# A mixer kernel's first loads: the 128 columns of x move from ACT's DMA queue to SP's

## The chip, the cores and the metric

The kernel runs on one core of a Trainium2 chip. The metric is the device time of one execution in microseconds (us); several executions are given by their median. The profile is that of one further execution.

The core has five engines that matter here: TensorE (PE), VectorE (DVE), ScalarE (ACT), GpSimd (POOL) and SyncE (SP). SP and ACT issue the loads and stores of this kernel, each on a queue of its own; in the profile SP's queue is q1 and ACT's is q10. The packets of both are moved by the same 16 DMA engines.

## The reference

The input x has 2048 rows of 512 bf16 values. Two branches read it, and a gate mixes them:

```python
# branch A: sliding, dilated local attention (32 heads of 16, 8 taps, 2 apart)
qkv = x @ wqkv                       # wqkv: 512 x 1536
logits = einsum(q, k[pos - 2*w]) * 16 ** -0.5     # w = 0..7, masked before the start
a = (softmax(logits) . v[pos - 2*w]) @ wo
# branch B: token mixing
h = layernorm(x)
u = gelu(h^T @ w1 + b1)              # w1: 2048 x 1792
b = (u @ w2 + b2)^T
# gate
g = sigmoid((x * gate_w).sum(-1))
out = g * a + (1 - g) * b
```

## The kernel before, in words

All of x, its transpose XT, the projections and the weights in use lie in one arena in SBUF. The work is written down as a list of operations, each with an engine, a planned duration, what it reads and writes, and at places an order by hand. A planner (`_Sched`) then puts the operations of each engine in order, with planned times, and works out which semaphores each must wait for. Each engine runs its own list in that order. Only the order and the waits reach the chip; the planned times do not.

The stages on TensorE follow one another:

- L536: warm-up matmuls on a constant, which nobody reads.
- L544: four small matmuls against an identity matrix. They transpose the 128 columns of x for the first 512 rows. ACT (`ev_tra`, L553) copies two results into XT, VectorE (`ev_trb`, L555) the other two.
- L617: the projections Q, K and V, 512 rows of x at a time ("blocks" 0 to 3). A result of 128 x 512 is the sum of four matmuls, one for each quarter of the 512 columns of x, which are the rows of Wq, Wk or Wv. ACT copies the results out (L625, L628).
- L696: sums over heads for the attention logits, from products that VectorE makes (L688).
- L810 and L860: the two big products of branch B. L876: the product with wo, whose results VectorE mixes into the output (L897).

For block 0 the eight results of Q and K lie in eight PSUM banks at once, and the loop goes over the quarters first: four matmuls (one for each quarter of Q's output) with column quarter 0 of x and the first quarter of Wq, then four with quarter 1, and so on, then Wk in two halves. So the first four matmuls need only 128 columns of x and 128 rows of Wq.

These 128 columns of block 0 come another way than the rest. The rest of block 0, columns 128 to 511, comes by a DMA that transposes on the way (`d_xt0`, L473). The first 128 columns come as a plain load, `d_xp` (512 rows of 256 bytes), into the tile OUTS, and TensorE transposes them (L544).

The first loads are, in the order in which they are issued before the change:

- on ACT's queue: `d_xp`, then the first quarter of Wq (`d_wp0_0`);
- on SP's queue: `d_xt0`, the other quarters of Wq (`d_wp0_1`, `d_wp0_2`, `d_wp0_3`), two halves of Wk (`d_wp1_0`, `d_wp1_2`), rows of x for the layer norm (`d_x0`), the transposing DMA of block 1 (`d_xt1`, L460), and then more of x, XT, Wv and w1.

Plain loads are issued at L429, through `mk_dma`. The loads on SP are kept in their order by `prev_dma()`: each is ordered behind the one before it. From `d_x2` on, `throttle()` makes each wait for the landing of the load five places ahead in the list `init_dmas`. The first loads carry planned landing times, set by hand, which stand in for the planner's own model of a DMA:

```python
for op_, t_ in zip(first_loads, (3.4, 4.6, 5.0, 5.4, 5.8, 6.6, 7.4, 8.2, 10.6)):
    op_.lands = t_
    op_.deps.clear()
d_xp.lands = 3.1
first_loads[0].order.add(d_xp)
```

`first_loads[0]` is the first quarter of Wq and `first_loads[1]` is `d_xt0`. The last line orders the quarter of Wq behind the columns of x on ACT's queue.

VectorE's whole order and parts of ACT's are written out as chains further down; the large matmuls of PE are one chain through `last_main`.

Of the kernel before, what the change touches and what calls it, by code (L numbers as in the profile page):

```python
# [333 lines left out]
def bass_gated_mix__sliding_local_dilated__mixer_token_mlp__prompt_kernel(nc, A_x, A_wqkv, A_wo, B_x, B_w1, B_b1, B_w2, B_b2, gate_w, out, dbg=None):  # L334
    with contextlib.ExitStack() as es:
# [3 lines left out]
        sch = _Sched()  # L339

        x2d = A_x[0]
        xv = x2d.rearrange("(t p) d -> p t d", p=128)
# [85 lines left out]
        def mk_dma(dst, src):  # L428
            return lambda e: e.dma_start(dst, src)  # L429
# [3 lines left out]
        def throttle():  # L433
            return [init_dmas[-5]] if len(init_dmas) >= 5 else []

        def prev_dma():
            return [init_dmas[-1]] if init_dmas else []

        def ld_x(t0, n, q="sp"):
            ds = sch.dsem("x%d" % t0)  # L440
            op = sch.dma(q, mk_dma(X[:, t0:t0 + n, :], xv[:, t0:t0 + n, :]), n * 128 * D * 2, ds,
                         writes=["x%d" % t for t in range(t0, t0 + n)], deps=throttle() if q == "sp" else [], after=prev_dma() if q == "sp" else [], name="d_x%d" % t0)
            if q == "sp":
                init_dmas.append(op)
            return op

        def ld_w(tn, d0, n, q="sp"):
            ds = sch.dsem("wqkv%d_%d" % (tn, d0))
            op = sch.dma(q, mk_dma(WQKV[:, d0:d0 + n, tn * D:(tn + 1) * D], wqkv_v[:, d0:d0 + n, tn * D:(tn + 1) * D]),
                         n * 128 * D * 2, ds, writes=["wqkv%d_%d" % (tn, dt) for dt in range(d0, d0 + n)],  # L450
                         deps=throttle() if q == "sp" and n == 4 else [], after=prev_dma() if q == "sp" else [],
                         issue=0.65 if n == 4 else 0.45, name="d_wp%d_%d" % (tn, d0))
            if q == "sp":
                init_dmas.append(op)
            return op
# [14 lines left out]
        def ld_xt0():  # L470
            ds = sch.dsem("xt0")
            dst = XT[:, 1:4, 0:512]
            op = sch.dma("sp", lambda e: e.dma_start_transpose(dst, x2d[0:512, 128:512]), 512 * 384 * 2, ds, issue=1.25,  # L473
                         writes=XT0[1:4], after=prev_dma(), name="d_xt0")
            init_dmas.append(op)
            return op

        XP = view("OUTS", BF16, [(128, 4), (1, 128)])
        d_xp = sch.dma("act", mk_dma(XP, xv[:, 0:4, 0:128]), 512 * 128 * 2, sch.dsem("xp"), writes=["outs0"], issue=0.4, name="d_xp")

        first_loads = [ld_w(0, 0, 1, "act"), ld_xt0(), ld_w(0, 1, 1), ld_w(0, 2, 1), ld_w(0, 3, 1), ld_w(1, 0, 2), ld_w(1, 2, 2),
                       ld_x(0, 2)]
        ld_xt(1)
        first_loads.append(init_dmas[-1])
        for op_, t_ in zip(first_loads, (3.4, 4.6, 5.0, 5.4, 5.8, 6.6, 7.4, 8.2, 10.6)):
            op_.lands = t_
            op_.deps.clear()
        d_xp.lands = 3.1
        first_loads[0].order.add(d_xp)
        init_dmas[:] = [first_loads[1]] + first_loads[5:]  # L490
        ld_x(2, 2)
        ld_x(4, 4)
# [7 lines left out]
        def ld_w1(j):  # L500
# [4 lines left out]
            if j < 4:  # L505
# [8 lines left out]
                       writes=["wo"], deps=throttle(), after=prev_dma(), name="d_wo")  # L514
# [4 lines left out]
        for i_, (v_, n_) in enumerate(((B_b1, NFT), (B_b2, NST))):  # L519
            vr = v_.rearrange("(t q j) -> q t j", q=4, j=32)  # L520
            for q_ in range(4):
                sch.dma("sp", mk_dma(psub(BR, 32 * q_, n_, 32 * i_, [(1, 32)]), vr[q_]), n_ * 64, ds_b, reads=["br"],
                        writes=["br_%d_%d" % (i_, q_)], deps=throttle(), after=prev_dma(), name="d_b_%d_%d" % (i_, q_), issue=0.45)
        d_w1.append(ld_w1(3))
        A("dve", lambda e: e.transpose(out=BT, in_=BR), 0.2, reads=["br_%d_%d" % (i_, q_) for i_ in range(2) for q_ in range(4)],
          writes=["btc"], name="t_b")
# [13 lines left out]
        def f_tr(h):  # L540
# [13 lines left out]
          writes=["xt0_0"], name="ev_tra", prio=0)  # L554
        A("dve", lambda e: e.tensor_copy(out=XT[:, 0, 256:512], in_=ps[:, 6, 0:256]), 0.35, reads=["lg6_0", "lg6_1"],  # L555
          writes=["xt0_0b"], name="ev_trb", prio=0)
# [76 lines left out]
        for (b0, d0, d1, s0, s1) in ((0, 0, 1, 0, 512), (0, 1, 2, 0, 512), (0, 2, 3, 0, 512), (0, 3, 4, 0, 512), (4, 0, 2, 0, 512), (4, 2, 4, 0, 512)):  # L633
            for b in range(b0, b0 + 4):
# [3 lines left out]
                                 writes=fbn[b], after=[last_main[0]], name="pf_%s%d_%d_%d" % (tnames[tn], dl, d0, s0))  # L638
                last_main[0].order.add(w3_)
        for b, (tn, dl) in enumerate(first):  # L640
            A("act", f_evq(tn, dl, 0, b), 0.52, reads=fbn[b] + (["k5pad"] if tn == 1 else []),
              writes=["%s5_%d_0" % (tnames[tn], dl)], name="ev_%s%d_0" % (tnames[tn], dl), prio=0)
# [7 lines left out]
        for (tn, dl, sb) in seq_proj:  # L650
# [4 lines left out]
                             writes=["acc%d" % bank], after=[last_main[0]], name="pj_%s%d_%d" % (tnames[tn], dl, sb), prio=0)  # L655
            A("act", f_evq(tn, dl, sb, bank), 0.62, reads=["acc%d" % bank] + (["k5pad"] if tn == 1 else ["v5pad"] if tn == 2 else []),
              writes=["%s5_%d_%d" % (tnames[tn], dl, sb)], name="ev_%s%d_%d" % (tnames[tn], dl, sb), prio=0)
# [11 lines left out]
                writes=["xa"] + ["wqkv%d_%d" % (tn, dt) for tn in range(3) for dt in range(4)], name="d_xa")  # L669
        for t in range(NST):  # L670
# [5 lines left out]
          writes=["th"], name="g_tanh", prio=0)  # L676
# [31 lines left out]
        for wh in range(2):  # L708
# [6 lines left out]
            for (dl, c0, nc_) in pieces:  # L715
# [5 lines left out]
                  writes=wr, name="qkm_%d_%d_%d" % (wh, dl, c0), prio=0)  # L721
            rd = sum([pbn(b_) for b_ in bufs], []) + PBX[wh] + ["rp"]
            for wl in range(4):
                qop = A("pe", f_qkr(list(enumerate(bufs)), (wl,)), 0.92, reads=rd, writes=["lg%d_0" % (4 + wl), "lg%d_1" % (4 + wl)],
                        name="qkr_%d_%d" % (wh, wl), prio=-100 + wl, delay=BURST_DELAY)
                A("act", (lambda wh_, wl_: (lambda e: e.activation(out=ATT[:, :, 4 * wh_ + wl_, :], in_=ps[:, 4 + wl_, :].rearrange("p (h c) -> p h c", h=2), func=AF.Copy)))(wh, wl),  # L726
                  0.55, reads=["lg%d_0" % (4 + wl), "lg%d_1" % (4 + wl)], writes=["lw%d" % (4 * wh + wl)],
                  name="lev_%d_%d" % (wh, wl), prio=0)
# [60 lines left out]
        for k_, u in enumerate(USEQ):  # L789
# [7 lines left out]
            for (nm, n_, du) in (("ava", 4, 2.25), ("avb", 2, 1.2)):  # L797
                A("dve", (lambda pv_, n__: (lambda e: e.tensor_tensor(out=pv_[:, 0:n__], in0=pv_[:, 0:n__], in1=pv_[:, n__:2 * n__], op=ALU.add)))(pv, n_),  # L798
                  du, writes=[pn], name="%s_%d" % (nm, u))
# [27 lines left out]
        for ft in range(NFT):  # L827
# [6 lines left out]
              name="gel_%d" % ft, prio=0)  # L834
# [84 lines left out]
        for i in range(NST):  # L919
# [4 lines left out]
            elif i > 1:  # L924
# [6 lines left out]
              name="t1_%d" % i, prio=0)  # L931
# [119 lines left out]
```

## Time and profile before

| | before |
|---|---|
| times of three runs | 169.61, 170.71, 167.72 us (median 169.61) |
| the profiled execution: time | 168.55 us |
| the profiled execution: span | 167.3 us |
| TensorE busy | 162.1 us, 97% of the span |
| VectorE busy | 151.3 us, 90% |
| ACT busy | 75.1 us, 45% |
| DMA packets on q1 (SP) | 45120 |
| DMA packets on q10 (ACT) | 2496 |

The span runs from the first to the last instruction of the profiled execution; its time also holds what lies around them. Times in the profile count from the span's start. A line of the profile gives the engine, the source line (L429), the operation and what it writes and reads; SPq and ACTq are the instruction streams of SP and ACT, in which DMAs are issued. The time that a DMA's issue takes there is not the time until its data has landed, which is given apart.

### The profile page before, as it was taken

What the parts mean: (1) busy time and instruction counts of PE and PEld (TensorE: products, weight loads), DVE (VectorE), ACT (ScalarE), POOL (GpSimd) and SP (SyncE); (2) the same over time, 40 slices, a digit from 0 to 9 for tenths busy, and PEclk for the clock granted to TensorE, in tenths of its full rate; (3) what the DMA queues carried; (4) which work ended last, traced back from release to release, by engine and by line L of the source; (5) the groups of instructions that cost most, each with busy time, mean ns of one, the idle gap of its engine ahead of it and who ended that gap; (6) DMA issues with size and microseconds to landing.
All of it is one profiled execution on the core that took longest, in us unless ns stands there. A gap on an engine that the chain in (4) does not pass through costs nothing.

```text
span 167.3 us, 2136 instructions
## 1 busy us (share of the span) xinstructions
PE 162.1 (97%) x845; PEld 77.5 (46%) x859; DVE 151.3 (90%) x154; ACT 75.1 (45%) x116; POOL 0.7 (0%) x8
## 2 busy tenths in 40 slices
PE   7699999999999999999999999999999999999994
PEld 2355555554454444444444444444444444444463
DVE  1055999999999999999999999999999999999896
ACT  3077688889899818793131121131231321310100
POOL 1000000000000000000000000000000000000000
PEclk9999999999999999999999999999999999999999
DMA  5999999959003846996779926462672570000454
GB/s 135 327 268 216 314 316 290 303 165 308 2 0 97 311 116 179 307 290 155 181 189 340 339 76 142 113 187 71 181 218 83 138 223 0 0 0 0 157 190 159
DMA packets 47625, 29.64 MB, mean 177 GB/s; under 512 B 9856, under 2 KB 46464, under 8 KB 47616
## 3 DMA queue, kind: packets, MB, share of 16 engines
q1 hardware_dynamic: 45120, 24.85, 54.4%
q10 hardware_dynamic: 2496, 4.66, 10.2%
q8 instruction: 7, 0.11, 0.3%
q14 instruction: 2, 0.02, 0.0%
HBM read 21.24 MB, written 2.10 MB: 140 GB/s over the span
## 4 chain that ended last, share of the span: by engine, by line
PE 91%; DMA 3%; DVE 2%; ACT 2%; issue 1%; ACTq 0%
PE ps L860 29%; PE ps L810 29%; PE ps L617 23%; PE ps L876 6%; PE ps L696 4%; DMA arena<-in_A_wqkv_dram 3%; DVE arena L897 2%; ACT L585 1%; ACT arena L628 1%; ACTq L429 0%; ACT arena L585 0%
## 5 line engine op out<-in xcount | busy, mean ns | idle before, releaser
L860 PE MATMUL ps<-arena 128*128 128x512 bf16 x220 | 48.5, 379 | 0.2
L810 PE MATMUL ps<-arena 128*128 128x512 bf16 x219 | 48.2, 379 | 0.4 <-issue 0.2
L617 PE MATMUL ps<-arena 128*128 128x512 bf16 x188 | 41.4, 379 | 1.6 <-DMA arena<-in_A_wqkv_dram 1.3
L688 DVE TENSOR_TENSOR arena<-arena 128x4096 bf16<-128x4096 bf16 (+1 forms) x12 | 35.5, 2998 | 2.5 <-ACT arena L628 2.1
L795 DVE TENSOR_TENSOR arena<-arena 128x8192 bf16<-128x8192 bf16 x8 | 35.0, 4419 | 0.0
L860 PEld LDWEIGHTS ps<-arena 128*128 128x128 bf16 x224 | 21.9, 98 | 26.4
L810 PEld LDWEIGHTS ps<-arena 128*128 128x128 bf16 x224 | 21.8, 98 | 26.6 <-ACT arena L726 0.4
L617 PEld LDWEIGHTS ps<-arena 128*128 128x128 bf16 x192 | 21.6, 113 | 21.5 <-issue 1.8
L928 ACT ACTIVATE arena<-ps,arena 128x512 bf16<-128x512 f32 x16 | 12.5, 778 | 39.4 <-PE ps L860 39.4
L798 DVE TENSOR_TENSOR arena<-arena 128x4096 bf16<-128x4096 bf16 (+1 forms) x16 | 27.0, 1751 | 0.0
L628 ACT ACTIVATE arena<-ps 128x512 bf16<-128x512 f32 x32 | 18.6, 596 | 4.5 <-PE ps L617 4.5
L831 ACT ACTIVATE arena<-ps,arena 128x512 bf16<-128x512 f32 x14 | 9.6, 687 | 22.2 <-PE ps L810 16.6
L572 DVE BATCH_NORM_STATS2 arena<-arena 128x6 f32<-128x512 bf16 x16 | 10.0, 682 | 6.1 <-DMA arena<-in_A_x_dram 6.1
L876 PE MATMUL ps<-arena 128*128 128x512 bf16 (+1 forms) x79 | 14.1, 336 | 0.1
L897 DVE SCALAR_TENSOR_TENSOR arena<-ps,arena 128x512 bf16<-128x512 f32 (+1 forms) x20 | 11.5, 637 | 0.9 <-PE ps L876 0.7
L596 ACT ACTIVATE arena<-arena 128x512 bf16<-128x512 bf16 x16 | 12.2, 804 | 0.0
L625 ACT ACTIVATE arena<-ps 128x512 bf16<-128x512 f32 x16 | 9.0, 597 | 6.2 <-PE ps L617 6.1
L876 PEld LDWEIGHTS ps<-arena 128*128 128x128 bf16 x80 | 7.8, 98 | 6.2
L672 DVE SCALAR_TENSOR_TENSOR arena<-arena 128x512 bf16<-128x512 bf16 x16 | 10.1, 689 | 0.0
L742 DVE TENSOR_TENSOR arena<-arena 128x512 bf16<-128x512 bf16 (+4 forms) x11 | 7.3, 667 | 0.6 <-ACT arena L761 0.2
L696 PE MATMUL ps<-arena 128*32 128x512 bf16 x128 | 7.3, 380 | 0.0
L726 ACT ACTIVATE arena<-ps 128x512 bf16<-128x512 f32 x8 | 4.7, 592 | 4.6 <-PE ps L696 4.6
(42 smaller groups left out, 40.0 us busy)
## 6 DMA issues: line engine op xcount, KB each, us to landing
arena<-in_B_w_dram SPq DMA_DIRECT2D x7, 1024.0 KB, 8.5
arena<-in_B_w_dram SPq DMA_DIRECT2D x8, 896.0 KB, 5.2
arena<-arena ACTq DMA_DIRECT2D x32, 128.0 KB, 2.9
arena<-in_A_x_dram SPq DMA_DIRECT2D x4, 512.0 KB, 6.1
out_dram<-arena SPq DMA_DIRECT2D x14, 128.0 KB, 1.7
arena<-in_A_x_dram SPq DMA_DIRECT2D x1, 1536.0 KB, 7.9
arena<-in_A_wqkv_dram SPq DMA_DIRECT2D x2, 256.0 KB, 3.8
arena<-in_A_x_dram SPq DMA_DIRECT2D x2, 256.0 KB, 3.6
```

The source lines that it names most:

```text
L596: A("act", (lambda t_: (lambda e: e.activation(out=X[:, t_, :], in_=X[:, t_, :], func=AF.Identity, scale=col(RSTD, t_), bias=col(NMR, t_)) ...
L617: ins = e.matmul(ps[:, bank, s0:s1], lhsT=lhsT, rhs=XT[:, dt, sb * 512 + s0:sb * 512 + s1], start=(dt == 0 and s0 == 0), stop=(dt == 3))
L628: return lambda e: e.activation(out=dst, in_=ps[:, bank, :], func=AF.Copy)
L688: return lambda e: e.tensor_tensor(out=PBL[buf][:, :, 512 * c0:512 * (c0 + nc_)], in0=in0, in1=in1, op=ALU.mult)
L696: ins = e.matmul(ps[32 * c:32 * c + 32, 4 + wl, :], lhsT=RP, rhs=PBL[buf][:, wl, c * 512:(c + 1) * 512], start=(dl == 0), stop=(dl == 3), ...
L795: A("dve", (lambda o_, i0, i1: (lambda e: e.tensor_tensor(out=o_, in0=i0, in1=i1, op=ALU.mult)))(pv, in0, in1), 4.4, reads=v_res + ["atx_% ...
L798: A("dve", (lambda pv_, n__: (lambda e: e.tensor_tensor(out=pv_[:, 0:n__], in0=pv_[:, 0:n__], in1=pv_[:, n__:2 * n__], op=ALU.add)))(pv, n ...
L810: ins = e.matmul(ps[:, bank, :], lhsT=W1W[:, slot, st, 128 * e_:128 * e_ + 128], rhs=X[:, st, :], start=(st == 0), stop=(st == NST - 1))
L860: ins = e.matmul(ps[:, bank, :], lhsT=W2S[slot][:, ft, 128 * e_:128 * e_ + 128], rhs=UT[:, ft, :], start=(ft == 0), stop=(ft == NFT - 1))
L876: ins = e.matmul(ps[:, bank, 0:c1 - c0], lhsT=OT[:, t, 128 * i:128 * i + 128], rhs=WO[:, t, c0:c1], start=(t == 0), stop=(t == 3))
L897: A("dve", (lambda i_, b_, c0_, c1_: (lambda e: e.scalar_tensor_tensor(out=T1[:, i_, c0_:c1_], in0=ps[:, b_, 0:c1_ - c0_], scalar=col(G, i ...
L928: A("act", (lambda i_, bank_: (lambda e: e.activation(out=T1[:, i_, :], in_=ps[:, bank_, :], func=AF.Identity, scale=col(OMG, i_), bias=co ...
```

## The change

`d_xp` is issued by SP instead of ACT, and `d_xt0` (`first_loads[1]`) is ordered behind it. The first quarter of Wq is then the only one of these loads on ACT's queue and has no load ahead of it. The planned landing of the Wq quarter goes from 3.4 to 3.0; those of the eight loads behind `d_xp` on SP go up by 0.3 each. Nothing else is changed.

```diff
         XP = view("OUTS", BF16, [(128, 4), (1, 128)])
-        d_xp = sch.dma("act", mk_dma(XP, xv[:, 0:4, 0:128]), 512 * 128 * 2, sch.dsem("xp"), writes=["outs0"], issue=0.4, name="d_xp")
+        d_xp = sch.dma("sp", mk_dma(XP, xv[:, 0:4, 0:128]), 512 * 128 * 2, sch.dsem("xp"), writes=["outs0"], issue=0.4, name="d_xp")
...
-        for op_, t_ in zip(first_loads, (3.4, 4.6, 5.0, 5.4, 5.8, 6.6, 7.4, 8.2, 10.6)):
+        for op_, t_ in zip(first_loads, (3.0, 4.9, 5.3, 5.7, 6.1, 6.9, 7.7, 8.5, 10.9)):
             op_.lands = t_
             op_.deps.clear()
         d_xp.lands = 3.1
-        first_loads[0].order.add(d_xp)
+        first_loads[1].order.add(d_xp)
         init_dmas[:] = [first_loads[1]] + first_loads[5:]
```

## The prediction

> **What bounds the kernel now.** I read the chain of work that ended last first, in order of time, then the waits of PE, then the table of stages, the timeline of the first six microseconds and the DMA landings of single issues.
>
> ```profile
> 0.74 0.06 issue
> 0.80 0.46 ACTq L429
> 1.25 0.03 issue
> 1.28 4.24 DMA arena<-in_A_wqkv_dram
> 5.52 0.09 issue
> 5.61 8.36 PE ps L617 x38
> ...
> 161.67 3.98 DVE arena L897 x9
> ```
>
> Columns are start, length, what. The chain starts with ACT issuing a load for 0.46 us (the 128 columns of x). Behind it ACT issues Wq's first quarter at 1.28, and PE stands until it lands at 5.52. After that it is TensorE nearly all the way to 161.7, and a VectorE tail.
>
> ```profile
> PE ps L617 <- DMA arena<-in_A_wqkv_dram: 1.3, 1, 1.3
> PE ps L536 <- PEq L1036: 0.8, 1, 0.8
> PE ps L617 <- ACT arena L585: 0.2, 1, 0.2
> PE ps L810 <- issue: 0.2, 1, 0.2
> ```
>
> These are all waits of PE that the profile lists: 1.3 us for that one landing, and 0.4 us later than the start.
>
> ```profile
> 2.00:5.60 3.60, 2.35 (x9) 0.77 (x8) 0.42 (x1) 1.51 (x2) 0.00 (x0) 1.00 1.13 285
> 5.60:12.50 6.90, 6.89 (x32) 3.64 (x33) 2.06 (x4) 3.14 (x7) 0.00 (x0) 1.00 1.09 292
> 12.50:161.70 149.20, 148.23 (x774) 69.88 (x787) 144.57 (x141) 70.25 (x109) 0.00 (x0) 1.00 0.63 172
> ```
>
> Behind the stretch and its length stand busy times of PE, PEld, DVE, ACT and POOL, then the granted clock, the DMA share and GB/s. From 5.6 on PE is busy 155.12 of 156.1 us, so what the start of the projections gains or loses goes through to the end. From 2.0 on the 16 DMA engines are full (shares of 1.13 and 1.09), so bytes ahead of a load count as well as its time of issue.
>
> ```profile
> 0.80 0.46 ACTq L429 DMA_DIRECT2D arena<-in_A_x_dram  x1
> 0.80 1.35 SPq L473 DMA_TRANSPOSE arena<-in_A_x_dram  x1
> 1.28 0.53 ACTq L429 DMA_DIRECT2D arena<-in_A_wqkv_dram  x1
> 2.22 2.49 SPq L429 DMA_DIRECT2D arena<-in_A_wqkv_dram  x5
> 3.33 0.58 PE L544 MATMUL ps<-arena 128*128 128x128 bf16 x4
> 3.74 0.38 ACT L553 ACTIVATE arena<-ps 128x256 bf16<-128x256 f32 x1 [0.62 <-PE ps L544]
> 3.96 0.42 DVE L555 CAST arena<-ps 128x256 bf16<-128x256 f32 x1 [2.45 <-PE ps L544]
> 5.27 3.36 SPq L460 DMA_TRANSPOSE arena<-in_A_x_dram  x1
> ```
>
> ```profile
> arena<-in_A_x_dram ACTq DMA_DIRECT2D x1, 128.0 KB, 2.4
> arena<-in_A_wqkv_dram ACTq DMA_DIRECT2D x1, 128.0 KB, 4.2
> arena<-in_A_x_dram SPq DMA_TRANSPOSE x1, 4.9
> arena<-in_A_wqkv_dram SPq DMA_DIRECT2D x1, 128.0 KB, 3.8
> ```
>
> The last number is us from issue to landing. The columns of x land at 3.2, the transposed rest at 5.7, Wq's first quarter at 5.5, its second (issued by SP at 2.22) at 6.0. The first four projection matmuls need the columns (transposed by L544, copied out by L553 and L555 until 4.38) and the first quarter; the next four need the transposed rest and the second quarter. Their pace: 16 L617 matmuls take 3.62 us, the last 0.38, so (3.62 - 0.38) / 15 = 0.216 each. The second four start at 5.61 + 4 x 0.216 = 6.47, 0.5 after their last input.
>
> **The change, part by part.**
>
> 1. Wq's first quarter is issued at 0.80 instead of 1.28 and has nothing ahead of it on ACT's queue. Fast end: the first load on that queue, of as many bytes, landed in 2.4, so 3.2. Slow end: its own 4.2, so 5.0. I take the row that stood in the same place, and add the 128 KB of the other queue's columns that now run beside it, 0.4 us at the 285 GB/s of this stretch: 3.6. Either end is before 5.52.
>
> 2. The columns of x are issued by SP at the same 0.80. Landing: 2.4 as now (3.2), or 0.4 later with Wq beside them (3.6). I take 3.4: the transposing matmuls and both copies move from 3.33 and 4.38 by some 0.25, and the copies end at 4.63. These copies, not Wq, are then what comes last for the first four, which start at 4.63 + 0.09 (as now from landing to matmul) = 4.7 instead of 5.61 and end at 5.6. Was Wq to take its slow end, they would start at 5.1.
>
> 3. The transposing DMA is issued at 1.28 instead of 0.80, and everything behind it on SP moves by the same 0.48: three quarters of Wq, two halves of Wk, block loads of x, the other transposing DMAs. What comes next for PE is the second quarter of Wq: issue at 2.70 instead of 2.22. Slow end: its 3.8 stays, 6.5. Fast end: it is the engines that set it; the bytes ahead of it (columns, Wq's first quarter, 384 KB transposed, itself: 768 KB) need 2.7 us at 285 GB/s from 2.0 on, 4.7, and 0.5 until the semaphore shows it (an estimate: the last packets of the columns' queue run out by 2.8, their landing is 3.2), so 5.2. I take its landing of today, 6.0: the engines are full before and after, and the bytes ahead of it are the same.
>
> 4. The sum. The second four start at the latest of 5.6 (the first four's end) and 6.0 + 0.05: 6.03 instead of 6.47, a gain of 0.44. Fast end: 5.6, a gain of 0.9. Slow end: 6.5, none. So of 1.3 us of wait at most 0.9 can come back, and I expect half of this; the rest turns into a second wait of 0.4 us between the first four and the second four, for SP's loads.
>
> 5. What costs nothing, and its cover. The third and fourth quarter are needed 0.86 and 1.73 after the second and land 0.2 and 0.6 after it (issued half a microsecond apart each, 3.4 and 3.3 to landing), so they stay covered. The second transposing DMA lands at 5.27 + 5.5 = 10.8; the 33rd matmul needs it at 5.61 + 32 x 0.216 = 12.5, with the shift and the gain 11.25 against 12.1: 0.8 is left. VectorE's statistics on the first x tiles come 0.48 later, but it then stands 2.1 us for ACT's copy (L688 waits for L628), so this is covered with about 1 us left. ACT's table load moves from 1.84 to about 1.4, and its first copy is at 3.74 or later. Planned landings only feed the planner: all loads behind the transposing DMA move by one and the same 0.3, and VectorE's order, the projections' order on PE and the SP loads' order are written as chains. I expect no other order.
>
> So: the profiled execution has a span of 167.3 and a time of 168.55; less 0.44 these are 166.8 and 168.1. The median shown, 169.61, lies 1.1 above that execution, and the three runs spread over 3 us, more than anything the change can do. I put the sum on the mean of the four executions known, (169.61 + 170.71 + 167.72 + 168.55) / 4 = 169.15: **168.7**.
>
> **The rivals.**
>
> A. SP's shift eats it all: transposing and second quarter land 0.48 later (6.2 and 6.5), the first four are early for nothing, the second four start at 6.5. Time: 169.2. For it: 4.9 and 3.8 are the only rows for these loads. Against it: the engines are full, so the queue is not all of it.
>
> B. Slower: the transposing DMA's issue gets long behind a plain load. With the queue empty L473 takes 1.35 us; L460, a third larger, takes 3.36 at 5.27 behind plain loads, where 1.8 would be in proportion. If the 512 short rows of the columns do this to L473, its issue takes 3.36 x 3/4 = 2.5, so 1.15 more, and the second quarter is issued at 2.22 + 0.48 + 1.15 = 3.85. With the shortest landing of SP's Wq loads, 3.3, it is there at 7.15 to 7.65 (3.8): the second four start 0.7 to 1.2 late. Time about 170.1. It decides once the second quarter lands after 6.5. Against it: only one load is ahead, not eight as before L460.
>
> C. TensorE's own pace. The L536 matmuls, as large as L617's, have weight loads at 1.22, 1.65, 2.08 and 2.50, so 0.43 apart, twice the 0.216. Somewhere between the last of them (3.71) and 5.61 the pace doubles, though the profile's granted clock says 1.00 in both. If it doubles only near 5.6, four matmuls from 4.7 on take 1.72 and end at 6.4: the gain is 0.05 to 0.1 and the time 169.1. If earlier, the sum stands. For it: the trace has no matmul in between. The Trainium skill (TensorE: Matmul & The Clock Gate, "Part 1: The HAM clock gate") says that the clock is halved until a window of about 3.4 us has been busy, and that the window runs free of the kernel's start; by that rule an earlier start buys slow matmuls in some runs, and the shorter stand of PE helps in others. The trace agrees on the factor of two; when it changes no row here shows.
>
> **How the numbers follow.** Forecast (a gain of 0.2 to 0.9, its own range 168.3 to 168.9): 0.5. A 0.2, B 0.15, C 0.15. All lie within 1.2 us of no change, and the runs' own spread is larger than that. The range goes from the fastest run less the largest gain, 167.72 - 0.9 = 166.8, to the slowest run without a gain, 170.8; B on top of a slow run is what is left out. 2% (3.4 us), about what a measurement of this kernel tells from no change, is more than twice the whole 1.3 us of wait, so faster has 0.04 and slower 0.04, for scatter and for an order that changes against my reading; the same 0.92.
>
> **What would show it.** Right: L617 starts at 4.6 to 4.9 and waits for VectorE's or ACT's copy; a second wait of PE at L617 of 0.2 to 0.6 for a DMA of SP; PE's first wait for Wq gone; the second transposing DMA still ahead of its matmuls. A: this second wait is 0.8 to 0.9. B: L473's issue is over 2 us long. C: the first L617 are 0.43 apart. Wrong altogether: Wq's first quarter still lands after 5, or the order on PE differs further down, or PE gets waits after 12 us that it has not now.

## The result and the profile after

The changed kernel takes 170.02 us (median of 20 runs, 168.86 to 170.76); the kernel before takes 168.25 in the same comparison (median of 20 runs: one of 292.1, the others 167.71 to 170.71). The ratio is 1.0101, with a 95% interval of 1.0078 to 1.0124: slower by 1%, where I had forecast faster by 0.3%. A ratio here leaves out the runs more than 1.5% above the fastest of their kernel, so it is not the quotient of the medians. The profiled execution after has a span of 169.3 and a time of 170.63, near the upper end of its runs.

The chain of work that ended last, after, in order of time (start, length, what):

```profile
0.80 3.10 DMA arena<-in_A_x_dram
3.90 0.14 issue
4.04 0.60 PE ps L544 x4
4.64 0.02 issue
4.66 0.44 DVE arena L555
5.10 0.05 issue
5.14 35.45 PE ps L617 x152
...
163.68 3.98 DVE arena L897 x9
```

Wq's quarter is gone from the chain, as forecast, and the projections start at 5.14 instead of 5.61. All the same the VectorE tail starts at 163.68 instead of 161.67. So 2.5 us are lost behind 5.14 (the 2.0 at the tail and the 0.47 of earlier start), and the waits of PE, after, do not hold them; this is the whole list:

```profile
PE ps L536 <- PEq L1036: 0.8, 1, 0.8
PE ps L544 <- DMA arena<-in_A_x_dram: 0.7, 1, 0.7
```

PE no longer waits for a load at L617. It waits 0.7 us ahead of the four small transposing matmuls, for the columns of x. Such idle time of TensorE is called a stand below. The table of stretches, after (busy time and number of instructions of PE, PEld, DVE, ACT, POOL; then granted clock, DMA share, GB/s):

```profile
5.14:10.16 5.02, 5.01 (x12) 1.76 (x13) 0.00 (x0) 0.00 (x0) 0.00 (x0) 1.00 0.98 251
10.16:15.00 4.84, 4.84 (x24) 2.53 (x23) 2.58 (x4) 3.63 (x8) 0.00 (x0) 1.00 1.13 269
```

Here the time is. In 5.02 us PE started 12 projection matmuls, in the next 4.84 us 23 of the same size (the row's 24 counts one that reaches over its start). PE counts as busy all through both, and the granted clock says 1.00 in both; the count tells, and so do the weight loads (PEld), one for each matmul:

```profile
9.40 0.15 PEld L617 LDWEIGHTS ps<-arena 128*128 128x128 bf16 x1 [0.28 <-issue]
9.82 0.15 PEld L617 LDWEIGHTS ps<-arena 128*128 128x128 bf16 x1 [0.28 <-issue]
10.21 4.86 PEld L617 LDWEIGHTS ps<-arena 128*128 128x128 bf16 x23 [0.24 <-issue]
```

They are 0.43 apart up to 10.2 and 0.216 from there on. 5.02 us at half pace cost 2.5 us; 0.47 of it the earlier start gives back, which leaves the 2.0.

The loads and the transposing, after, from the timeline:

```profile
0.80 0.43 ACTq L429 DMA_DIRECT2D arena<-in_A_wqkv_dram  x1
0.80 0.45 SPq L429 DMA_DIRECT2D arena<-in_A_x_dram  x1
1.31 2.10 SPq L473 DMA_TRANSPOSE arena<-in_A_x_dram  x1
3.47 2.50 SPq L429 DMA_DIRECT2D arena<-in_A_wqkv_dram  x5
4.04 0.59 PE L544 MATMUL ps<-arena 128*128 128x128 bf16 x4 [0.69 <-DMA arena<-in_A_x_dram]
4.66 0.42 DVE L555 CAST arena<-ps 128x256 bf16<-128x256 f32 x1 [3.16 <-PE ps L544]
```

And the landings of the first two of them, after (the last number is us from issue):

```profile
arena<-in_A_wqkv_dram ACTq DMA_DIRECT2D x1, 128.0 KB, 2.7
arena<-in_A_x_dram SPq DMA_DIRECT2D x1, 128.0 KB, 3.1
```

Wq's quarter lands at 3.45 instead of 5.52. The columns land at 3.90 instead of 3.20. The transposing DMA's issue takes 2.10 instead of 1.35, so the loads behind it on SP are issued 1.25 later (3.47 against 2.22), not 0.48.

### The profile page after: what moved, and what is told of

Same layout as the page of the kernel before. It is cut to its first block, busy times and chain, and to the rows that moved or that the text cites. A ratio compares the mean times of both kernels' runs of the same rounds, so it can differ in the third digit from the quotient of the medians.

```text
span 169.3 us, 2150 instructions
## 1 busy us (share of the span) xinstructions
PE 165.5 (98%) x859; PEld 78.0 (46%) x859; DVE 151.3 (89%) x154; ACT 75.1 (44%) x116; POOL 0.7 (0%) x8
## 4 chain that ended last, share of the span: by engine, by line
PE 94%; DVE 3%; DMA 2%; issue 0%
PE ps L810 29%; PE ps L860 29%; PE ps L617 26%; PE ps L876 6%; PE ps L696 4%; DVE arena L897 2%; DMA arena<-in_A_x_dram 2%; PE ps L544 0%; DVE arena L555 0%
## 5 line engine op out<-in xcount | busy, mean ns | idle before, releaser
L810 PE MATMUL ps<-arena 128*128 128x512 bf16 x224 | 48.7, 379 | 0.0
L860 PE MATMUL ps<-arena 128*128 128x512 bf16 x224 | 48.7, 379 | 0.0
L617 PE MATMUL ps<-arena 128*128 128x512 bf16 x192 | 44.3, 394 | 0.1
L617 PEld LDWEIGHTS ps<-arena 128*128 128x128 bf16 x192 | 22.0, 115 | 22.5 <-issue 3.3
```

The costliest lines, as they stand in the source:

```text
L617: ins = e.matmul(ps[:, bank, s0:s1], lhsT=lhsT, rhs=XT[:, dt, sb * 512 + s0:sb * 512 + s1], start=(dt == 0 and s0 == 0), stop=(dt == 3))
L810: ins = e.matmul(ps[:, bank, :], lhsT=W1W[:, slot, st, 128 * e_:128 * e_ + 128], rhs=X[:, st, :], start=(st == 0), stop=(st == NST - 1))
L860: ins = e.matmul(ps[:, bank, :], lhsT=W2S[slot][:, ft, 128 * e_:128 * e_ + 128], rhs=UT[:, ft, :], start=(ft == 0), stop=(ft == NFT - 1))
```

## The experiments

I tested two theories. **G**: TensorE's stand ahead of the transposing matmuls puts off its full pace. **Q**: SP's loads are late, by the shift and by the longer issue of L473.

**The changed kernel with the stand filled by two more warm-up matmuls.**

```diff
-        A("pe", f_warm(5), 2.13, writes=["lg7_0", "lg7_1"], name="warm1", prio=-100)
+        A("pe", f_warm(7), 2.13, writes=["lg7_0", "lg7_1"], name="warm1", prio=-100)
```

> The changed kernel with seven instead of five warm-up matmuls, so that TensorE does not stand for 0.70 us ahead of the transposing matmuls at 4.04; loads and queues as in the changed kernel. Theory G (the stand in the warm-up keeps TensorE at half pace until about 10): the L617 weight loads are 0.216 apart from the first four or eight on, the first four start at 5.1 as in the changed kernel, the second four at 6.2 (second quarter of Wq at 6.15), and the time is about 2.0 below the changed kernel: 167.7 to 168.2, 0 to 0.5 below the kernel before. Theory Q (SP's loads are late: L473's issue takes 2.10 instead of 1.35, the second quarter and all behind it is later): nothing changes against the changed kernel, 169.8 to 170.3.

Measured: 169.02 us (168.43 to 169.37), ratio to the kernel before 1.0019 (0.9986 to 1.0051). That is 1.0 below the changed kernel, half of what G promised, and not the "nothing changes" of Q. Its runs spread over 0.9 us, those of the changed kernel over 1.9. TensorE's timeline, with seven warm-ups:

```profile
5.14 4.02 PE L617 MATMUL ps<-arena 128*128 128x512 bf16 x16
9.63 5.59 PE L617 MATMUL ps<-arena 128*128 128x512 bf16 x25 [0.48 <-DMA arena<-in_A_wqkv_dram]
```

The projections start at the same 5.14, and now 16 of them are through in 4.02 us: in this profile the pace doubles near 6 instead of at 10.2, by nothing but dummy work ahead of it. But a new wait follows, for Wk's first half: PE idles 0.48, and the seventeenth matmul starts at 9.63. At the pace of 0.216 it would have started at 8.99, so the delay is 0.64. (The 0.85 in the next expectation is the distance to the start of the sixteenth; and the list of PE's waits holds no second wait, for the transposing DMA.) So both theories have a part.

**The kernel before with seven warm-ups**, the other half of that pair: work on TensorE alike up to the projections, only the queues differ. The edit is the same line, in the kernel before.

> The kernel before with seven warm-up matmuls: the same work on TensorE up to the first projection as in the changed kernel with seven, the transposing matmuls at about 4.0 in both, only the queues differ. Theory G+Q (two parts: the stand in the warm-up, and SP's later loads, which cost PE two waits of 0.85 for Wk's first half and 0.15 for the second transposing DMA): no such waits here, Wk's first half lands by 8.0, time 167.8 to 168.4, so 0.6 to 1.0 below the changed kernel with seven (169.02). Theory G alone: as the changed kernel with seven, 168.8 to 169.2.

Measured: 168.29 (167.81 to 168.82), ratio 0.9977 (0.9943 to 1.0011). TensorE's timeline:

```profile
3.99 0.63 PE L544 MATMUL ps<-arena 128*128 128x128 bf16 x4
4.42 0.63 PE L536 MATMUL ps<-const-bfloat16-1.0 128*128 128x512 bf16 x1
5.14 9.04 PE L617 MATMUL ps<-arena 128*128 128x512 bf16 x40
```

The same starts, at 3.99 and 5.14, and then 40 matmuls without a wait. The landing of Wk's first half, in the changed kernel with seven (issued at 4.92) and in this one (issued at 3.76):

```profile
arena<-in_A_wqkv_dram SPq DMA_DIRECT2D x1, 256.0 KB, 4.7
arena<-in_A_wqkv_dram SPq DMA_DIRECT2D x1, 256.0 KB, 3.5
```

It landed at 7.3 here and at 9.6 in the other. By the medians Q's part is 169.02 - 168.29 = 0.73 and G's part is 170.02 - 169.02 = 1.00. Together with the 0.04 between this kernel and the one before they make the 1.77 between the medians. These medians come from separate series of runs, in which the kernel before had medians of 168.18 to 168.37, so the parts are good to some 0.2. The two profiles differ by more, 1.2 us of span: beside the 0.64 of the wait, the pace doubled near 5.2 here and near 6 in the other, which is worth 0.4.

**The kernel before with a stand made by taking warm-ups away** (the same line with `f_warm(3)`).

> The kernel before, its queues untouched, with three instead of five warm-up matmuls, so that TensorE stands for some 0.9 us ahead of the transposing matmuls at 3.33. Theory G: L617 starts at 5.6 as before, but its weight loads are 0.43 apart for 3 to 6 us; the time goes up by 1.5 to 3.0, to 169.8 to 171.3. Theory Q: the loads are those of the kernel before, so 168.0 to 168.4.

Measured: 169.46 (168.44 to 170.69), ratio 1.0051 (1.0015 to 1.0088). Slower with the queues untouched, as G says and Q does not, though by less than I expected. In its profile PE stands 0.76 ahead of the transposing matmuls and starts the projections at 4.57, since Wq's quarter landed at 4.5, and not at 5.6; the pace doubles at 6.9.

**The changed kernel with six warm-ups**, a stand of 0.2 (the same line with `f_warm(6)`).

> The changed kernel with six warm-up matmuls: TensorE stands for about 0.27 us ahead of the transposing matmuls instead of 0.70. Theory G: in between; if a short stand is forgiven, 167.7 to 168.3 as with seven, if each stand starts the count anew, 169 to 170. Theory Q: 169.8 to 170.3.

Measured: 169.03 (168.68 to 169.21), ratio 1.0031 (1.0003 to 1.0059): outside the range of 167.7 to 168.3 that forgiveness was to give, but no worse than with seven. In its profile the pace doubles at 3.80, as the stand begins (3.77 to 3.96), so this profile does not show whether a short stand is forgiven. That none of the twelve runs is above 169.21 speaks for it. What keeps the time up in the profile is Q's part, which that range had left out: PE waits 0.57 ahead of the second four (6.49) for Wq's second quarter, and 0.22 at 12.93 for the second transposing DMA, both loads of SP.

**The two loads exchanged**: the columns first on ACT, Wq's quarter first on SP.

```diff
-        d_xp = sch.dma("sp", ...)
+        d_xp = sch.dma("act", ...)
-        first_loads = [ld_w(0, 0, 1, "act"), ld_xt0(), ...
+        first_loads = [ld_w(0, 0, 1, "sp"), ld_xt0(), ...
-        first_loads[1].order.add(d_xp)
+        first_loads[1].order.add(first_loads[0])
```

> The two loads exchanged: the columns of x alone and first on ACT's queue, the first quarter of Wq first on SP's queue, in front of the transposing DMA; five warm-up matmuls. SP's queue is delayed as in the changed kernel. Theory G: what counts is when the columns land. If at 3.2 as in the kernel before, the transposing matmuls follow the warm-up without a stand, L617 starts at 4.4 to 4.6 at full pace or gets it within 1 us, second four at 6.1 to 6.5, time 167.8 to 168.4. If they land at 3.9 because Wq's quarter runs beside them on the DMA engines, the stand is there again and the time is 169.5 to 170.3. Theory Q: 169.8 to 170.3 wherever the columns land.

Measured: 169.81 (168.96 to 170.26), ratio 1.0065 (1.0034 to 1.0097). The columns landed at 3.83, from ACT's queue too, so it is not SP's queue that delays them. The stand is there (the transposing matmuls start at 3.97), and the pace doubles at 8.5. The time does not part the theories, since both forecast it; the landing is what this run adds.

**The same with seven warm-ups.**

> The exchanged loads (Wq's first quarter first on SP in front of the transposing DMA, the columns first on ACT) with seven warm-up matmuls, so that TensorE does not stand ahead of the transposing matmuls. If any plain load in front of the transposing DMA on SP is what makes the loads behind it late, this is as the changed kernel with seven: Wk's halves land at 8.0 to 9.6 and 9.7 to 10.3, PE waits once or twice for SP's loads behind the second four, 168.7 to 169.2. If it was the 512 short rows of the columns in SP's queue, the loads are earlier and the time is 168.1 to 168.5, as the kernel before with seven (168.29).

Measured: 168.81 (168.32 to 169.10), ratio 1.0035 (1.0013 to 1.0058). The time is where the first case had it, its reason is not: L473's issue took 1.51, Wk's halves landed at 7.9 and 9.1, and PE did not wait for them in this profile. So a quarter of Wq in front of the transposing DMA makes SP's loads less late than the 512 short rows do: Wk's first half landed at 7.9 and 8.0 in the two profiles of this order, at 8.9 to 9.8 in the five of the changed kernel with five, six and seven warm-ups. What makes the 0.5 over the kernel before with seven warm-ups (168.81 against 168.29) stays open.

**All first loads on SP, Wq's quarter behind the transposing DMA**, so that the columns have nothing beside them.

```diff
-        first_loads = [ld_w(0, 0, 1, "act"), ld_xt0(), ld_w(0, 1, 1), ...
+        f1_ = ld_xt0(); first_loads = [ld_w(0, 0, 1), f1_, ld_w(0, 1, 1), ...
```

> The columns of x first on SP and alone in flight: Wq's first quarter is issued by SP behind the transposing DMA, ACT issues none of the first loads. Five warm-up matmuls. If it is Wq's quarter beside them that delays the columns (3.9 instead of 3.2 in the changed kernel), they land at 3.1 to 3.3 here; if it is SP's queue, at 3.8 to 3.9. If a plain load ahead of it on SP lengthens the issue of L473, it takes about 2 us here too; if Wq's packets do, 1.35. Time 169 to 171, as Wq's first quarter lands late, near 6.

Measured: 170.47, one run; Wq's first quarter landed at 6.15. Its timeline and, in the second fence, the landing of its first load:

```profile
0.80 0.45 SPq L429 DMA_DIRECT2D arena<-in_A_x_dram  x1
1.31 1.68 SPq L473 DMA_TRANSPOSE arena<-in_A_x_dram  x1
3.05 0.57 SPq L429 DMA_DIRECT2D arena<-in_A_wqkv_dram  x1
```

```profile
arena<-in_A_x_dram SPq DMA_DIRECT2D x1, 128.0 KB, 2.4
```

Alone, the columns land 2.4 after their issue from SP as well. It is Wq's quarter in flight beside them that makes it 3.1. The issue of L473 fell between my two cases: 1.35 with nothing ahead, 1.68 behind the columns, 2.10 behind the columns with Wq's quarter beside.

**Wq's quarter first on ACT, the columns behind it, SP as before**, with nine warm-ups.

```diff
-        first_loads[0].order.add(d_xp)
+        d_xp.order.add(first_loads[0])
-        A("pe", f_warm(5), 2.13, ...
+        A("pe", f_warm(9), 2.13, ...
```

> One part of the change alone, Wq's first quarter first on ACT's queue, and the columns of x behind it on the same queue; SP's queue as in the kernel before. Nine warm-up matmuls, so that TensorE does not stand. Theory Q (the transposing DMA's longer issue behind a plain load delays all of SP's loads): L473's issue is 1.35 again and Wk's first half lands by 8.0, without a wait for it. The columns land at 4.4 to 5.5, as the second load of ACT's queue did, the second four start at 6.4 to 7.2, time 168.3 to 169.3. If Wk's first half still lands after 8.9, it is Wq's early packets and not SP's queue.

Measured: 169.41 (168.79 to 169.67), ratio 1.0054 (1.0028 to 1.0080). The median is 0.1 above the range forecast. L473's issue took 1.34 and Wk's first half landed at 8.0, although Wq's early packets were there as in the changed kernel: the lateness belongs to SP's queue. (That no projection waited for it says less, as they start 1.4 later here.) The loads of ACT's queue, with the transposing DMA of SP:

```profile
arena<-in_A_wqkv_dram ACTq DMA_DIRECT2D x1, 128.0 KB, 2.3
arena<-in_A_x_dram ACTq DMA_DIRECT2D x1, 128.0 KB, 4.3
arena<-in_A_x_dram SPq DMA_TRANSPOSE x1, 4.9
```

The second load on ACT's queue landed at 5.5 and not 0.5 behind the first. Here it is the columns, and they hold up the transposing matmuls until 5.64. So TensorE did stand, for 1.16 us, but behind the doubling (near 3.8), and it kept its full pace: the projections start at 6.55 and are 0.216 apart from the second on.

**The changed kernel, two further profiles.**

> The changed kernel once more, for a second profile. Theory G with a window that runs free of the kernel's start: the pace of L617 doubles at another time than 10.2, somewhere between 6.8 and 10.3, and the time is 170.6 less half of the difference (within 0.3), not below 168.9. If the time of doubling hangs on the kernel's own start, it is at 10.2 again and the time 170.4 to 170.8.

> The changed kernel, third profile. As for the second: doubling between 6.8 and 10.3 and the time 170.6 less half of the difference to 10.2 under the free window; 10.2 and 170.4 to 170.8 if it hangs on the start.

Measured: 169.90 with the doubling at 8.9, and 169.42 with the doubling near 7.1. So it does not hang on the kernel's own start. For the first, half of the difference gives 170.6 - 0.65 = 169.95. For the second it gives 169.1, and 0.3 is missing. Its weight loads show most of it (start, length, count, idle time before):

```profile
7.21 2.06 PEld L617 LDWEIGHTS ps<-arena 128*128 128x128 bf16 x10 [0.17 <-issue]
9.80 3.17 PEld L617 LDWEIGHTS ps<-arena 128*128 128x128 bf16 x16 [0.53 <-DMA arena<-in_A_wqkv_dram]
13.29 1.66 PEld L617 LDWEIGHTS ps<-arena 128*128 128x128 bf16 x9 [0.32 <-ACT arena L628]
```

As soon as the pace comes early, Wk's late half holds up the weight loads until 9.80; the seventeenth matmul starts at 9.81 instead of 9.59, 0.2 late. The changed kernel has two limits one behind the other: a run that escapes the half pace runs into the late loads.

**The kernel before, a second profile.**

> The kernel before, second profile. In the three other kernels with its queues Wq's first quarter landed at 4.5 to 4.6 and not at 5.52: if the profile that the prediction was made from was an unusual one, it lands at 4.4 to 4.7 here, L617 starts at 4.5 to 4.7, and the time is 167.7 to 168.3 if TensorE gets its full pace by 5. If 5.5 is usual for it, L617 starts at 5.6.

Measured: 168.58. Its weight loads:

```profile
4.64 0.14 PEld L617 LDWEIGHTS ps<-arena 128*128 128x128 bf16 x2 [0.90 <-DVE arena L555]
...
6.34 0.15 PEld L617 LDWEIGHTS ps<-arena 128*128 128x128 bf16 x1 [0.28 <-issue]
6.71 6.37 PEld L617 LDWEIGHTS ps<-arena 128*128 128x128 bf16 x30 [0.23 <-issue]
```

Wq's quarter landed at 4.58 and the first matmul of L617 starts at 4.67, in the kernel before, so there was no wait of 1.3 for it (PE's list has 0.3). The pace doubles near 6.7, which is why its time is not under 168.3.

**The kernel before with two more fillers behind the transposing matmuls.**

```diff
-        w3_ = A("pe", f_warm(1), 0.43, writes=["lg7_0", "lg7_1"], after=[tr_], name="warm3", prio=-100)
+        w3_ = A("pe", f_warm(3), 0.43, writes=["lg7_0", "lg7_1"], after=[tr_], name="warm3", prio=-100)
```

> The kernel before with three instead of one filler matmul behind the transposing ones, which shortens the stand of TensorE between 4.3 and the landing of Wq's first quarter (4.5 to 5.5). Theory G: fewer runs are at half pace for long; most runs 167.7 to 168.4 as before, the ones near 170 become rare; the median is 0 to 0.4 below the kernel before. If it is the stand ahead of the transposing matmuls alone that counts, nothing changes. Theory Q: nothing changes.

Measured: 168.10 (12 runs from 167.66 to 168.70), against 168.37 of the kernel before (29 runs from 167.69 to 170.41); ratio 0.9977 (0.9946 to 1.0008). In its profile the projections start at 4.63 at full pace, and its span of 166.4 is the shortest of all that were profiled. It is the version that the experiments point to: it keeps the old queues, and in its profile TensorE does not stand behind its start. Its gain is not clear of no change. None of its 12 runs is near 170, where 5 of the 29 of the kernel before are (170.05 to 170.41), as Theory G forecast; twelve runs are few for that, and no profile shows what held up those five.

## When the pace doubles

In seven of the profiles the trace's record of the clock gives the moment. I worked out, from the starts and ends of the matmuls, how busy PE was in the 3.4 us up to it and in the 3.4 us before that. In the other seven there is no such record, and the distance of the matmuls and their weight loads has to tell.

| kernel | doubling at, us | busy share up to it | busy share before that |
|---|---|---|---|
| before, first profile | 4.48 | 0.96 | 0.07 |
| before, three warm-ups | 6.86 | 0.91 | 0.54 |
| after, first profile | 10.16 | 1.00 | 0.77 |
| after, second profile | 8.87 | 1.00 | 0.83 |
| after, six warm-ups | 3.80 | 0.86 | 0.00 |
| loads exchanged | 8.51 | 1.00 | 0.79 |
| all on SP | 8.94 | 0.79 | 0.64 |

The doubling comes at the end of a stretch that is busy for at least 0.79, and the stretch ahead of it was never busier than 0.83. The length of 3.4 us is that of the Trainium skill (TensorE: Matmul & The Clock Gate, "Part 1: The HAM clock gate"), which says that a window of that length runs free of the kernel and must be busy. The runs agree: the doubling lies between 7.1 and 10.2 in three profiles of one and the same kernel. The length shows too: the trace's records of full pace last 160.43 us in five of the seven and 163.84 in the other two, 3.41 apart. How busy is busy enough, these seven do not settle. A share of 0.79 was enough with all loads on SP, one of 0.83 was not in the second profile after, and the ends of matmuls are modelled; if there is a limit, it lies near four fifths. With a stand of 0.7 at 3.3 to 4.0, a window that holds it whole has a share of at most 0.79 (1 - 0.7 / 3.4), and the next one ends up to 3.4 us later. That this is how the stand puts off the doubling is argued. That it does, all fourteen profiles show: in the five with a stand of 0.5 to 0.8 us ahead of the transposing matmuls the pace doubled at 6.9 to 10.2, in the seven with at most 0.2 there at 3.8 to 6.7. Of the other two, Wq's quarter first on ACT doubled near 3.8, ahead of its stand, and all loads on SP had 1.94 us ahead of L617 and doubled at 8.94.

## Why the prediction was wrong, step by step

Two terms that the prediction put at nothing decided: a stand of TensorE ahead of the transposing matmuls (step 2), 1.00 of the median, and SP's later loads behind the second quarter of Wq (step 5), 0.73.

- **What bounds the kernel** (an early gain or loss at L617 goes through to the end): right. The 2.5 us lost up to the doubling, less the earlier start, are the 2.0 at the end of the chain.
- **Step 1** (Wq's quarter at 3.6 instead of 5.5): right, 3.45.
- **Step 2** (the columns at 3.4, 3.6 at most): mis-sized. They landed at 3.90; what I charged for Wq beside them, 0.2 of 0.4, was 0.75 (3.90 against 3.15 alone). And this is where the prediction failed: I moved the transposing matmuls by 0.25 and asked only what waits for them, not what TensorE does meanwhile. It stood for 0.69 us in the middle of its warm-up, and ran at half pace until 10.16.
- **Step 3** (second quarter of Wq at 6.0, between 5.2 and 6.5): right, 6.15. SP's shift was 1.25 and not 0.48, as L473's issue grew, but the load then landed 2.7 after its issue instead of 3.8. That fits the reason given, that the engines and the bytes ahead set it; that the two differences cancel so closely is luck.
- **Step 4** (second four at 6.03): in the profile with seven warm-ups they start at 6.4, no gain to speak of against 6.47. In the changed kernel itself they start at 6.83.
- **Step 5** (what costs nothing): wrong for the loads behind. I checked the cover of the second transposing DMA with a shift of 0.48 (0.8 left) and did not check Wk's halves. Wk's first half landed at 9.59 with seven warm-ups and held the seventeenth matmul up by 0.64. That one wait is near the 0.73 of theory Q. That it makes the whole of it is not shown: the exchanged loads with seven warm-ups lose 0.5 without such a wait in their profile. The cover that I did check was short as well: with six warm-ups PE waited 0.22 for the second transposing DMA, which landed at 12.79 and not at 11.25.
- **Rival B** (L473's issue grows behind a plain load): its mechanism was there, 2.10 where I wrote 2.5; it told at another load than I named, Wk's half instead of Wq's second quarter. That its time of 170.1 is so near the 170.02 measured is luck: the wait that it was made of did not come. (Ahead of L460 stand six plain loads and the first transposing DMA, not eight loads.)
- **Rival C** (TensorE's pace) named the right mechanism with the wrong price. I let it eat the gain (169.1). The trace's record puts the doubling of that profile at 4.48, ahead of the 4.7 that I forecast for the projections, so by its own condition the sum stood. I took the moment of doubling as fixed, and did not see that the change itself moves it, by a stand in the stretch that has to be busy. Its price was 1.0 of the median and 2.5 in the profiled run.
- **The base**: the profile of before was unusual in the one row that I built on. Wq's quarter landed at 5.52 in it, and at 4.5 to 4.6 in four other profiles with these queues and the same loads. The wait that the change was to remove is mostly not there. And the level that I added the gain to, 169.15, lies 0.9 above the median of the kernel before, 168.25.
- The range held 170.02 by the scatter of the runs that I had allowed for; the one case that I had worked out near it, B, was not what happened.

Open: why Wk's half takes 4.7 from issue to landing with the columns in SP's queue (changed kernel, seven warm-ups) and 3.5 without (kernel before, seven warm-ups), beyond being issued 1.2 later; what costs the exchanged loads with seven warm-ups 0.5; and why Wq's quarter landed late in one profile of five.

## What to carry to other kernels

Matmuls ahead of the real work are part of the path when the pace depends on them: before a load is moved that they wait for, ask whether TensorE would stand, and put a dummy matmul into the hole. Read the pace from the distance of weight loads, not from busy shares. And before a wait is priced, see in a second profile whether it is there at all.

## What the runs showed of the hardware

- TensorE's pace doubled between 3.8 and 10.2 us after the start, by how busy it had been, and the profile's granted clock read 1.00 on both sides of the doubling. With a stand of 0.5 to 0.8 us inside the warm-up it came at 6.9 to 10.2; a stand of 1.16 us behind it cost no pace.
- Two loads of 128 KB, issued at the same moment on two queues, do not both land in the time of one: the columns took 2.4 alone and 2.9 to 3.2 beside Wq's quarter, from either queue; Wq's quarter took 2.5 to 2.7 beside them, and 2.3 where it was issued 0.4 ahead of them.
- The issue of the same transposing DMA took 1.34 to 1.36 us with nothing ahead of it on its queue, 1.68 behind the 512 short rows of the columns alone, 1.51 and 1.82 behind Wq's quarter with the columns beside on the other queue, and 1.85 to 2.13 behind the columns with Wq's quarter beside.
